# Loading and folding the first weights by quarters, with the first transposes in the softmax gap

## The chip, the cores and the metric

The kernel runs on one core of a Trainium2 chip. The time is the device time of one execution, in microseconds (us), from repeated executions; all of them here are marked "fast" (none is more than 1.5% above the fastest of its kernel). The traces give a span that is some 2 us shorter than the time (573.6 us for the kernel before), and all times of day below are counted from the start of that span. PE is the matrix engine (TensorE) and PEld its weight load, ACT is ScalarE, DVE is VectorE, POOL is GpSimd, which issues the loads. A "line" such as L345 is a line of that kernel's own source, so the same code has slightly different lines before and after.

## The reference, cut to what matters

```python
qn = q / (norm(q, axis=1) + 1e-6);  kn = k / (norm(k, axis=1) + 1e-6)   # q, k, v: 4 x 5824 x 256
A = softmax(kn.transpose(0, 2, 1) @ qn / tau)                          # 256 x 256, one per batch
x = (v @ A).reshape(23296, 256)
out = ((x @ w1) * (x @ w2) @ w3) @ w_out                               # w1, w2: 256 x 1024
```

The kernel uses that (v @ A) @ w1 equals v @ (A @ w1). It computes A for a batch, **folds** it into w1 and w2 (tiles `Wf`), and then multiplies rows of v by the folded weights. Before the first folds there is nothing for PE to do with v.

## The kernel before

A fold is two matmuls of 512 columns (over the two halves of the 256 contracted rows) and an eviction (a copy by ScalarE or VectorE out of PSUM, where the matmuls put their results) that scales by the reciprocal row sums. PSUM buffers carry tags: "ab" has four, "out" three, and each tag hands its buffers out in turn.

```python
def fold_mm(i, c2, tag="ab", on_act=None):
    ...                                              # w, c1, h from i; 512 columns
    nc.tensor.matmul(st["fold", i], lhsT=st["e"][:, c2, ...], rhs=w12[:, c2, w, h*512:(h+1)*512], ...)
    if c2 == CT - 1:                                 # evict, scaled: ScalarE or VectorE
        ...
def first_folds():
    sum_mm(0); fold_mm(0, 0); fold_mm(1, 0)          # need the first half of e
    sum_mm(1); fold_mm(0, 1); fold_mm(1, 1)          # need the second
    fold(2)
    transpose_half_on_pe(0, 0, 0, False)             # 8 transposes of v, tag "out"
    fold(3, on_act=True)
    fold(4, "out", on_act=False); fold(5, "out")
```

The loads behind q and k, all issued by GpSimd, and the end of the softmax:

```python
for h in range(2):                                   # w1, w2 by halves of 512 columns
    nc.gpsimd.dma_start(out=w12[:, :, 0, hs], in_=w1r[:, :, hs])
    nc.gpsimd.dma_start(out=w12[:, :, 1, hs], in_=w2r[:, :, hs])
    if h == 0: new_piece("v", 0, 0)
    load_part("v", 0, 0, h * half, (h + 1) * half)
load_piece("v", 0, 1); load_piece("v", 0, 2)
nc.gpsimd.dma_start(out=wout_sb, ...); nc.gpsimd.dma_start(out=w3_bf, in_=w3r)
...
soft0[3]()        # scaled scores and exp: gives e
busy(4)           # four filler matmuls
soft0[4]()        # first_folds
```

Everything later is placed by a planned clock: each piece of work has a planned time and cost, and is emitted between the products a = v Wf1 and b = v Wf2. Later loads also wait for earlier work: a one-element GpSimd copy ("gate", "hold") reads a tile, so that the loads after it are not issued before that tile is there.

```python
for i in range(2):
    at(1.5 + 0.6 * i, 0.43, soft0[5 + i])            # the last two folds, among the first products
```

Of the kernel before, what the change touches and what calls it, by code (L numbers as in the profile page):

```python
# [10 lines left out]
AF = mybir.ActivationFunctionType  # L11
ALU = mybir.AluOpType
F32 = DT.float32
BF16 = DT.bfloat16

P = 128
PIECE = 8
# [7 lines left out]
def kernel(  # L25
# [12 lines left out]
    nc = tc.nc  # L38
# [3 lines left out]
    F = moe_w1.shape[1]  # L42
# [6 lines left out]
    CT = C // P  # L49
# [18 lines left out]
    psum = ctx.enter_context(tc.tile_pool(name="psum", bufs=1, space=bass.MemoryType.PSUM))  # L68
# [15 lines left out]
    w12 = consts.tile([P, CT, 2, F], BF16)  # L84
# [15 lines left out]
    def new_piece(nm, n, pi):  # L100
        t = in_pool.tile([P, PIECE, C], BF16, tag=nm, name=f"{nm}_{n}_{pi}", bufs=IN_BUFS[nm])
        pieces[nm, n, pi] = t
        if pi == NP_ - 1:
            if nm != "v":
                nc.vector.memset(t[LEFT:, LAST, :], 0.0)
            nc.gpsimd.dma_start(out=t[:LEFT, LAST, :], in_=qk_main[nm, n][1])

    def load_part(nm, n, pi, lo, hi):
        nc.gpsimd.dma_start(  # L109
            out=pieces[nm, n, pi][:, lo:hi, :], in_=qk_main[nm, n][0][:, pi * PIECE + lo : pi * PIECE + hi, :]  # L110
        )

    def load_piece(nm, n, pi, cuts=()):

        new_piece(nm, n, pi)
        ends = [0, *cuts, LAST if pi == NP_ - 1 else PIECE]
        for lo, hi in zip(ends, ends[1:]):
            load_part(nm, n, pi, lo, hi)
# [3 lines left out]
    def new_vT(n):  # L122
        vTs[n] = (
            vT_pool.tile([P, NT - 1, CT, P], BF16, tag="vT", name=f"vT_{n}"),
            vT_pool.tile([P, CT, P + LEFT], BF16, tag="vTt", name=f"vTt_{n}"),
        )

    def pe_transpose(dst, src, tag, on_act):

        m = psum.tile([P, 8, P], BF16, tag=tag, name=f"tr_{nc.get_next_instruction_name()}", bufs={"ab": 4, "out": 3}[tag])  # L130
        for i, blk in enumerate(src):
            nc.tensor.transpose(m[:, i, :], blk, ident_b)
        if on_act:
            nc.scalar.copy(dst, m)
        else:
            nc.vector.tensor_copy(dst, m)

    def transpose_half_on_pe(n, pi, h, on_act):
        if pi == 0 and h == 0:
            new_vT(n)  # L140
        t = pieces["v", n, pi]
        i0 = 4 * h
        pe_transpose(
            vTs[n][0][:, pi * PIECE + i0 : pi * PIECE + i0 + 4, :, :].rearrange("p i c t -> p (i c) t"),
            [t[:, i0 + i, ct * P : (ct + 1) * P] for i in range(4) for ct in range(CT)],
            "out", on_act,
        )
# [17 lines left out]
    Wf = {}  # L165
# [39 lines left out]
    def busy(k):  # L205

        m = psum.tile([P, 512], F32, tag="ab", name=f"warm_{nc.get_next_instruction_name()}", bufs=4)
        for _ in range(k):
            nc.tensor.matmul(m, lhsT=warm[:, :P], rhs=warm, start=True, stop=True, skip_group_check=True)
# [29 lines left out]
    def soft_units(n):  # L239
        st = {}  # L240
# [93 lines left out]
            sum_mm(0)  # L334
            sum_mm(1)

        def fold_mm(i, c2, tag="ab", on_act=None):
            h, rest = divmod(i, 4)
            w, c1 = divmod(rest, 2)
            if c2 == 0:  # L340
                st["fold", i] = psum.tile(
                    [P, 512], F32, tag=tag, name=f"fold_{n}_{i}", bufs={"ab": 4, "out": 3}[tag]
                )
            nc.tensor.matmul(  # L344
                st["fold", i], lhsT=st["e"][:, c2, c1 * P : (c1 + 1) * P], rhs=w12[:, c2, w, h * 512 : (h + 1) * 512],  # L345
                start=(c2 == 0), stop=(c2 == CT - 1),
            )
            if c2 == CT - 1:
                dst = Wf[n][:, c1, w, h * 512 : (h + 1) * 512]
                if on_act if on_act is not None else i % 2 == 0:  # L350
                    nc.scalar.activation(out=dst, in_=st["fold", i], func=AF.Copy, scale=st["rs"][:, c1 : c1 + 1])  # L351
                else:
                    nc.vector.tensor_scalar_mul(dst, st["fold", i], st["rs"][:, c1 : c1 + 1])

        def fold(i, tag="ab", on_act=None):
            fold_mm(i, 0, tag)
            fold_mm(i, 1, tag, i % 2 == 0 if on_act is None else on_act)

        def first_folds():
            sum_mm(0)  # L360
            fold_mm(0, 0)
            fold_mm(1, 0)
            sum_mm(1)
            fold_mm(0, 1)
            fold_mm(1, 1)
            fold(2)
            transpose_half_on_pe(0, 0, 0, False)
            fold(3, on_act=True)
            fold(4, "out", on_act=False)
            fold(5, "out")  # L370

        if n == 0:
            return [k_first, k_row, q_first, scaled_first, first_folds] + [lambda i=i: fold(i) for i in range(6, 8)]
        head = [(0.0, norms), (0.5, k_row), (0.4, q_sums)]
        return head + [(0.0, scaled), (0.2, sums)] + [(0.43, lambda i=i: fold(i)) for i in range(8)]

# [13 lines left out]
    def at(t, cost, fn):  # L390
        seq[0] += 1
        agenda.append((t, seq[0], cost, fn))
# [105 lines left out]
    half = PIECE // 2  # L498
# [18 lines left out]
    w1r = moe_w1.rearrange("(ch cl) f -> cl ch f", cl=P)  # L517
    w2r = moe_w2.rearrange("(ch cl) f -> cl ch f", cl=P)
# [6 lines left out]
    soft0 = soft_units(0)  # L525
    whole = range(PIECE)
    lo, hi = range(half), range(half, PIECE)
# [10 lines left out]
        squares("q", pi, whole)  # L538
        products(pi, whole)
    load_piece("q", 0, 5, (1, 3, 4))  # L540
    for h in range(2):
        hs = slice(h * F // 2, (h + 1) * F // 2)
        nc.gpsimd.dma_start(out=w12[:, :, 0, hs], in_=w1r[:, :, hs])
        nc.gpsimd.dma_start(out=w12[:, :, 1, hs], in_=w2r[:, :, hs])
        if h == 0:
            new_piece("v", 0, 0)
        load_part("v", 0, 0, h * half, (h + 1) * half)
    load_piece("v", 0, 1)
    load_piece("v", 0, 2)
    nc.gpsimd.dma_start(out=wout_sb, in_=moe_w_out.rearrange("(lh ll) c -> ll lh c", ll=P))  # L550
# [14 lines left out]
        if i == 0:  # L565
            soft0[1]()
    soft0[3]()
    busy(4)
    soft0[4]()
    w_ready = [False]  # L570

# [15 lines left out]
    def make_agenda(b):  # L587
        agenda.clear()
        clock[0] = 0.0
        n = b + 1  # L590
        if b == 0:
            for i in range(2):
                at(1.5 + 0.6 * i, 0.43, soft0[5 + i])
            at(4.0, 0.5, lambda: transpose_half_on_pe(0, 0, 1, False))
            at(7.0, 0.5, lambda: transpose_half_on_pe(0, 1, 0, True))
            at(8.0, 0.5, lambda: transpose_half_on_pe(0, 1, 1, False))
            at(15.0, 0.0, transpose_w3)
            at(15.0, 0.0, lambda: transpose_piece(0, 2))
            for jt in range(FT):
                at(26.0 + 1.2 * jt, 0.87, lambda jt=jt: w_unit(jt))  # L600
            moves = [("v", 0, 3, 29.0), ("qk", 1, 0, 38.0), ("qk", 1, 1, 43.0), ("v", 0, 4, 50.0), ("qk", 1, 2, 58.0)]
            moves += [("qk", 1, 3, 63.0), ("v", 0, 5, 70.0), ("qk", 1, 4, 81.0), ("qk", 1, 5, 87.0)]
            moves += [("v", 1, 0, 96.0), ("v", 1, 1, 106.0), ("v", 1, 2, 116.0), ("qk", 2, 0, 126.0)]
            t0, t1 = 58.0, 120.0
        else:
            moves = [("v", b, 3, 1.0), ("qk", n, 1, 10.0), ("qk", n, 2, 17.0), ("v", b, 4, 26.0), ("qk", n, 3, 38.0)]
            moves += [("v", b, 5, 46.0), ("qk", n, 4, 58.0), ("qk", n, 5, 66.0)]
            moves += [("v", n, 0, 76.0), ("v", n, 1, 86.0), ("v", n, 2, 96.0), ("qk", n + 1, 0, 108.0)]
            moves = [m for m in moves if m[1] < B]
            t0, t1 = 16.0, 104.0  # L610

        before = (0, 2) if b == 0 else None
        for nm, m, pi, t in moves:
            if before is not None:
                at(t, 0.0, lambda w=before: hold(vTs[w[0]][1][:1, 0, :1] if w[1] == NP_ - 1 else vTs[w[0]][0][:1, w[1] * PIECE, 0, :1]))
            at(t, 0.0, gate)
            if nm == "qk":
                at(t, 0.0, lambda m=m, pi=pi: load_qk(m, pi))
                before = None
            else:  # L620
                at(t, 0.0, lambda m=m, pi=pi: load_piece("v", m, pi))
                at(t + 4.0, 0.0, lambda m=m, pi=pi: transpose_piece(m, pi))
                before = (m, pi)
        if n == B:
            agenda.sort()
            return
        units = score_units(n)
        for i, (cst, fn) in enumerate(units):
            at(t0 + (t1 - t0) * i / len(units), cst, fn)
        soft = soft_units(n)  # L630
        ts = [t1 + 1.0, t1 + 3.5, t1 + 4.0, t1 + 8.0, t1 + 12.0] + [t1 + 13.0 + 0.9 * i for i in range(8)]
        for t, (cst, fn) in zip(ts, soft):
            at(t, cst, fn)
        agenda.sort()
# [50 lines left out]
```

## Time and profile before

| | kernel before |
|---|---|
| time, median of the first three runs | 575.47 us (575.47 to 576.11) |
| span | 573.64 us |
| first softmax sum on PE | 37.00 us |
| first product a | 40.15 us |
| last wait of PE for a load | 32.66 us |

PE is busy for 98% of the span, and from 37.00 us on nearly without a hole. So the place to look is the order of its instructions near 37 us, which the prediction shows. These lines are from the timeline of GpSimd in the kernel before: start, duration, engine, line, operation, tiles, count.

```profile
29.73 0.70 POOL L543 DMA_DIRECT2D w<-in_moe_w_dram  x1 [0.73 <-DMA q<-in_q_dram]
30.42 0.72 POOL L544 DMA_DIRECT2D w<-in_moe_w_dram  x1
31.49 0.54 POOL L109 DMA_DIRECT2D v<-in_v_dram  x1 [0.35 <-DMA k<-in_k_dram]
...
35.19 0.93 POOL L550 DMA_DIRECT2D w_wout<-in_moe_w_out_dram  x1
```

The first halves of w1 and w2 are issued ahead of v, and w_out's issue, the first of the long ones, falls at 35.2 us, in the middle of the softmax.

### The profile page before, as it was taken

Reading aid. Unit: us, or ns where it says so; the run is one execution under the profiler, and the core shown is the slowest. Engines: PE = TensorE matmul, PEld = TensorE weight load, DVE = VectorE, ACT = ScalarE, POOL = GpSimd, SP = SyncE. Lnnn points to the kernel's source line nnn. Section 1 sums busy time; section 2 is a strip of 40 time slices with the busy share of each in tenths; the row PEclk is TensorE's granted clock in tenths of the full one; section 3 lists DMA queues with packets and bytes.
Section 4 is the critical chain, followed back from the end, with each engine's and each line's share of the span. In section 5 each row is a group of like instructions: output and inputs, shape, how many; then the busy total and the mean of one; then the engine's idle time right before and its main releaser. Section 6 shows DMA issues by size and latency. Waiting matters only on the chain.

```text
span 573.6 us, 10125 instructions
## 1 busy us (share of the span) xinstructions
PE 561.9 (98%) x3760; PEld 357.0 (62%) x3766; DVE 374.1 (65%) x597; ACT 337.9 (59%) x624; POOL 71.0 (12%) x162
## 2 busy tenths in 40 slices
PE   8789999999999999999999999999999999999997
PEld 4755576776666666666666666666665666666665
DVE  0047744787967567887776567778876656565564
ACT  0046534777766567776765567767765555454453
POOL 5240020202010111221000012021100000000000
PEclk9999999999999999999999999999999999999999
DMA  8999959779574696495661596675740325221011
GB/s 163 211 194 208 188 99 235 175 171 213 134 185 108 123 207 151 95 190 120 147 147 49 117 192 143 132 142 119 184 110 38 85 74 146 63 63 74 38 71 59
DMA packets 74561, 76.93 MB, mean 134 GB/s; under 512 B 54161, under 2 KB 58257, under 8 KB 74513
## 3 DMA queue, kind: packets, MB, share of 16 engines
q0 software_dynamic: 15504, 39.46, 39.2%
q1 hardware_dynamic: 58784, 36.64, 21.1%
q8 instruction: 29, 0.48, 0.3%
q10 hardware_dynamic: 224, 0.20, 0.1%
q14 instruction: 20, 0.16, 0.1%
HBM read 78.91 MB, written 23.86 MB: 179 GB/s over the span
## 4 chain that ended last, share of the span: by engine, by line
PE 91%; DMA 5%; ACT 1%; issue 1%; DVE 1%; POOL 1%; ACTq 0%; POOLq 0%
PE o L466 27%; PE a L425 27%; PE b L425 27%; PE G L188 5%; DMA k<-in_k_dram 3%; PE fold L344 2%; DMA q<-in_q_dram 2%; PE w L575 1%; ACT as L431 1%; POOL k L109 0%; PE row L272 0%; POOL q L109 0%; DVE abs L440 0%; DVE osb L487 0%; ACT kr L276 0%
## 5 line engine op out<-in xcount | busy, mean ns | idle before, releaser
L440 DVE TENSOR_TENSOR abs<-as,b 128x512 bf16<-128x512 bf16 x336 | 229.7, 685 | 140.5 <-ACT as L431 128.7
L431 ACT CAST as<-a 128x512 bf16<-128x512 f32 (+1 forms) x384 | 215.4, 562 | 177.7 <-PE a L425 86.7
L425 PEld LDWEIGHTS <-Wf 128*128 128x128 bf16 x1536 | 149.1, 98 | 102.5 <-issue 2.6
L466 PE MATMUL o<-W_sb,abs 128*128 128x256 bf16 x1376 | 209.7, 273 | 0.5 <-ACT osb L486 0.4
L425 PE MATMUL a<-vT,Wf 128*128 128x512 bf16 x704 | 209.4, 379 | 0.4
L425 PE MATMUL b<-vT,Wf 128*128 128x512 bf16 x704 | 209.4, 379 | 0.0
L466 PEld LDWEIGHTS <-abs 128*128 128x128 bf16 x1376 | 134.5, 98 | 82.0 <-issue 0.6
L197 DVE TENSOR_TENSOR acc<-acc,sq 128x1024 f32<-128x1024 f32 x66 | 80.4, 1219 | 0.8 <-ACT sq L185 0.8
L188 PE MATMUL G<-k,q 128*128 128x256 bf16 x276 | 49.6, 273 | 0.0
L185 ACT ACTIVATE sq<-q 128x512 f32<-128x512 bf16 x66 | 41.8, 633 | 0.0
L185 ACT ACTIVATE sq<-k 128x512 f32<-128x512 bf16 x66 | 41.6, 630 | 0.0
L413 POOL COPY gate_t<-abs 1x1 bf16<-1x1 bf16 x39 | 12.1, 310 | 183.7 <-DVE abs L440 183.1
L487 DVE COPY osb<-o 128x512 f32<-128x512 f32 x44 | 30.1, 684 | 0.0
L188 PEld LDWEIGHTS <-q 128*128 128x128 bf16 x276 | 27.0, 98 | 3.1
L486 ACT COPY osb<-o 128x512 f32<-128x512 f32 x44 | 25.7, 585 | 4.6 <-PE o L466 2.6
L417 POOL COPY gate_t<-vT 1x1 bf16<-1x1 bf16 x17 | 4.0, 234 | 180.5 <-DMA vT<-v 145.1
L274 ACT ACTIVATE kr<-row 128x256 f32<-128x256 f32 x4 | 1.5, 384 | 34.0 <-PE row L272 34.0
L109 POOL DMA_DIRECT2D q<-in_q_dram x29 | 15.6, 538 | 12.5 <-DMA k<-in_k_dram 5.2
L344 PE MATMUL fold<-w,e 128*128 128x512 bf16 x61 | 16.5, 378 | 0.1
L351 ACT ACTIVATE Wf<-fold,rs 128x512 bf16<-128x512 f32 x16 | 10.9, 687 | 7.2 <-PE fold L344 4.3
L109 POOL DMA_DIRECT2D k<-in_k_dram x25 | 13.7, 550 | 3.9 <-DMA k<-in_k_dram 1.9
L109 POOL DMA_DIRECT2D v<-in_v_dram x25 | 13.4, 539 | 4.0 <-issue 2.6
(87 smaller groups left out, 219.1 us busy)
## 6 DMA issues: line engine op xcount, KB each, us to landing
out_dram<-osb SPq DMA_DIRECT2D x44, 512.0 KB, 3.1
k<-in_k_dram POOLq DMA_DIRECT2D x19, 512.0 KB, 8.8
v<-in_v_dram POOLq DMA_DIRECT2D x19, 512.0 KB, 5.1
q<-in_q_dram POOLq DMA_DIRECT2D x18, 512.0 KB, 6.5
w_wout<-in_moe_w_dram POOLq DMA_DIRECT2D x1, 2048.0 KB, 22.9
k<-in_k_dram POOLq DMA_DIRECT2D x4, 320.0 KB, 9.4
v<-in_v_dram POOLq DMA_DIRECT2D x4, 320.0 KB, 5.2
q<-in_q_dram POOLq DMA_DIRECT2D x4, 256.0 KB, 11.9
```

The source lines that it names most:

```text
L109: nc.gpsimd.dma_start(out=pieces[nm, n, pi][:, lo:hi, :], in_=qk_main[nm, n][0][:, pi * PIECE + lo : pi * PIECE + hi, :])
L185: nc.scalar.activation(out=dst[:, :, part, :], in_=src[:, o : o + 2, :], func=AF.Square)
L188: nc.tensor.matmul(G[:, ct, :], lhsT=qt[:, i, ct * P : (ct + 1) * P], rhs=kt[:, i, :], start=(pr == 0 and part == 0 and ct == 0), stop=(pr ...
L197: nc.vector.tensor_add(accs[n], accs[n], sqs[0])
L344: nc.tensor.matmul(st["fold", i], lhsT=st["e"][:, c2, c1 * P : (c1 + 1) * P], rhs=w12[:, c2, w, h * 512 : (h + 1) * 512], start=(c2 == 0), ...
L413: nc.gpsimd.tensor_copy(gate_t, last_ab[0][:1, :1])
L425: nc.tensor.matmul(t[:, :n], lhsT=Wf[b][:, ct, w, j * P : (j + 1) * P], rhs=rhs_of(b, c, ct), start=(ct == 0), stop=(ct == CT - 1),)
L431: nc.scalar.copy(a_sb[:, :n], tiles[0][:, :n])
L440: nc.vector.tensor_mul(ab, a_sb, tiles[1])
L466: nc.tensor.matmul(tl[h][:, o, :], lhsT=lhsT, rhs=W_sb[:, j, :], start=(j == 0 and o == 0), stop=(j == FT - 1 and (small or o == 1)), skip ...
L486: nc.scalar.copy(o[:, 0:2, :], tl[0])
L487: nc.vector.tensor_copy(o[:, 2:4, :], tl[1])
```

## The change

Its intent: have v there earlier and transpose it while PE waits for the softmax; make the first folds, their evictions and their loads smaller, so that the first products can start sooner.

```diff
-        def fold_mm(i, c2, tag="ab", on_act=None):            # 512 columns
+        def fold_mm(key, c2, tag="ab", on_act=True):          # key = (w, c1, lo, hi)
...
         def first_folds():
             sum_mm(0)
-            fold_mm(0, 0); fold_mm(1, 0)
+            for c1 in range(CT): fold_mm((0, c1, 0, 256), 0)
             sum_mm(1)
-            fold_mm(0, 1); fold_mm(1, 1); fold(2)
-            transpose_half_on_pe(0, 0, 0, False)
-            fold(3, on_act=True)
-            fold(4, "out", on_act=False); fold(5, "out")
+            for c1 in range(CT): fold_mm((0, c1, 0, 256), 1, on_act=c1 == 0)
+            for w, lo in ((1, 0), (0, 256), (1, 256)):
+                for c1 in range(CT):
+                    for c2 in range(CT):
+                        fold_mm((w, c1, lo, lo + 256), c2, "ab" if lo == 0 else "out", c1 == 0)
...
-    for h in range(2): ...                                    # w halves, v between
+    new_piece("v", 0, 0)
+    load_part("v", 0, 0, 0, half)
+    for f0, f1 in ((0, 256), (256, 512), (512, F)):
+        nc.gpsimd.dma_start(out=w12[:, :, 0, f0:f1], in_=w1r[:, :, f0:f1])
+        nc.gpsimd.dma_start(out=w12[:, :, 1, f0:f1], in_=w2r[:, :, f0:f1])
+    load_part("v", 0, 0, half, PIECE)
...
-    busy(4)
+    busy(3)
+    transpose_half_on_pe(0, 0, 0, False)
     soft0[4]()
...
-            for i in range(2):
-                at(1.5 + 0.6 * i, 0.43, soft0[5 + i])
+            for i in range(4):
+                at(0.8 + 0.6 * i, 0.43, soft0[5 + i])
```

More of the change, by code (lines that the diff above doesn't have):

```diff
@@ L335, in sums @@
             sum_mm(1)
-        def fold_mm(i, c2, tag="ab", on_act=None):
-            h, rest = divmod(i, 4)
-            w, c1 = divmod(rest, 2)
+        def fold_mm(key, c2, tag="ab", on_act=True):
+            w, c1, lo, hi = key
             if c2 == 0:
-                st["fold", i] = psum.tile(
-                    [P, 512], F32, tag=tag, name=f"fold_{n}_{i}", bufs={"ab": 4, "out": 3}[tag]
+                st[key] = psum.tile(
+                    [P, 512], F32, tag=tag, name=f"fold_{n}_{w}_{c1}_{lo}", bufs={"ab": 4, "out": 3}[tag]
                 )
+            m = st[key][:, : hi - lo]
             nc.tensor.matmul(
-                st["fold", i], lhsT=st["e"][:, c2, c1 * P : (c1 + 1) * P], rhs=w12[:, c2, w, h * 512 : (h + 1) * 512],
+                m, lhsT=st["e"][:, c2, c1 * P : (c1 + 1) * P], rhs=w12[:, c2, w, lo:hi],
                 start=(c2 == 0), stop=(c2 == CT - 1),
@@ L348, in fold_mm, with fold @@
             if c2 == CT - 1:
-                dst = Wf[n][:, c1, w, h * 512 : (h + 1) * 512]
-                if on_act if on_act is not None else i % 2 == 0:
-                    nc.scalar.activation(out=dst, in_=st["fold", i], func=AF.Copy, scale=st["rs"][:, c1 : c1 + 1])
-                else:
-                    nc.vector.tensor_scalar_mul(dst, st["fold", i], st["rs"][:, c1 : c1 + 1])
-        def fold(i, tag="ab", on_act=None):
-            fold_mm(i, 0, tag)
-            fold_mm(i, 1, tag, i % 2 == 0 if on_act is None else on_act)
+                dst = Wf[n][:, c1, w, lo:hi]
+                if on_act:
+                    nc.scalar.activation(out=dst, in_=m, func=AF.Copy, scale=st["rs"][:, c1 : c1 + 1])
+                else:
+                    nc.vector.tensor_scalar_mul(dst, m, st["rs"][:, c1 : c1 + 1])
+        def fold(i, tag="ab"):
+            h, rest = divmod(i, 4)
+            w, c1 = divmod(rest, 2)
+            for c2 in range(CT):
+                fold_mm((w, c1, h * 512, (h + 1) * 512), c2, tag, i % 2 == 0)
         def first_folds():
             sum_mm(0)
-            fold_mm(0, 0)
-            fold_mm(1, 0)
+            for c1 in range(CT):
+                fold_mm((0, c1, 0, 256), 0)
             sum_mm(1)
-            fold_mm(0, 1)
-            fold_mm(1, 1)
-            fold(2)
-            transpose_half_on_pe(0, 0, 0, False)
-            fold(3, on_act=True)
-            fold(4, "out", on_act=False)
-            fold(5, "out")
+            for c1 in range(CT):
+                fold_mm((0, c1, 0, 256), 1, on_act=c1 == 0)
+            for w, lo in ((1, 0), (0, 256), (1, 256)):
+                for c1 in range(CT):
+                    for c2 in range(CT):
+                        fold_mm((w, c1, lo, lo + 256), c2, "ab" if lo == 0 else "out", c1 == 0)
         if n == 0:
-            return [k_first, k_row, q_first, scaled_first, first_folds] + [lambda i=i: fold(i) for i in range(6, 8)]
+            return [k_first, k_row, q_first, scaled_first, first_folds] + [lambda i=i: fold(i) for i in range(4, 8)]
         head = [(0.0, norms), (0.5, k_row), (0.4, q_sums)]
@@ L540 @@
     load_piece("q", 0, 5, (1, 3, 4))
-    for h in range(2):
-        hs = slice(h * F // 2, (h + 1) * F // 2)
-        nc.gpsimd.dma_start(out=w12[:, :, 0, hs], in_=w1r[:, :, hs])
-        nc.gpsimd.dma_start(out=w12[:, :, 1, hs], in_=w2r[:, :, hs])
-        if h == 0:
-            new_piece("v", 0, 0)
-        load_part("v", 0, 0, h * half, (h + 1) * half)
+    new_piece("v", 0, 0)
[4 more added lines that the diff above has]
+    load_part("v", 0, 0, half, PIECE)
     load_piece("v", 0, 1)
```

## The prediction

> **What bounds the kernel now.** I read the page's engine shares first, then who TensorE (PE) waited for, then the order of its work around the place that the change touches.
>
> ```profile
> PE 561.9 (98%) x3760; PEld 357.0 (62%) x3766; DVE 374.1 (65%) x597; ACT 337.9 (59%) x624; POOL 71.0 (12%) x162
> ...
> PE sqq L221 <- DMA q<-in_q_dram: 4.2, 4, 2.0
> PE warm_I-91_92 L209 <- DVE warm L78: 1.3, 1, 1.3
> PE sum L323 <- ACT e L307: 1.0, 1, 1.0
> PE o L466 <- ACT osb L486: 0.4, 1, 0.4
> ...
> 37.00:40.15 3.15, 3.15 (x24) 1.70 (x25) 2.00 (x5) 2.27 (x4) 0.18 (x1) 1.00 1.15 191
> 40.15:80.00 39.85, 39.85 (x240) 22.34 (x239) 26.98 (x42) 22.84 (x41) 0.90 (x3) 1.00 0.95 176
> ```
>
> The reader sees a PE that is busy for 98% of 573.6 us, and whose waits (us in total, times, longest) come almost all before 37 us: loads of q, the warm-up, and 1.0 us for the first softmax result e. From 37.00 us on (a row of stretches gives bounds, length, PE busy) it has no hole. So for the first 37 us loads and then a softmax chain set the pace; after that **the sum of PE's own instructions does**, and a microsecond more or less of PE work or PE waiting just after 37 us should move the end by as much. The change works exactly there:
>
> ```profile
> 34.98 1.03 PE L209 MATMUL warm_I-479_480<-warm 128*128 128x512 bf16 x3
> 37.00 0.20 PE L323 MATMUL sum<-ones_b,e 128*128 128x1 bf16 x2 [1.00 <-ACT e L307]
> 37.07 0.59 PE L344 MATMUL fold<-w,e 128*128 128x512 bf16 x2
> 37.50 0.19 PE L323 MATMUL sum<-ones_b,e 128*128 128x1 bf16 x2
> 37.55 1.02 PE L344 MATMUL fold<-w,e 128*128 128x512 bf16 x4
> 38.41 0.61 PE L132 MATMUL tr_I-508_509<-ident_b,v 128*128 128x128 bf16 x8
> 38.86 1.46 PE L344 MATMUL fold<-w,e 128*128 128x512 bf16 x6
> 40.15 0.59 PE L425 MATMUL a<-vT,Wf 128*128 128x512 bf16 x2
> ```
>
> Starts, not durations, are to be differenced, because matmuls overlap: 12 folds and 8 transposes stand between the softmax (37.00) and the first a (40.15). The transposes take 38.86 - 38.41 = 0.45 us of that, and one 512-column fold matmul 0.216 us (6 in 40.15 - 38.86).
>
> **What the Trainium skill says.** (1) "TensorE: Matmul & The Clock Gate", section "Wait — 56ns, not 53.3ns?": a warm matmul's start-to-start time is its columns at 2.4 GHz plus about 2.5 ns. Two of 256 columns then cost one of 512, less 2.5 ns the other way. The trace agrees: eight 256-column w matmuls advance the chain by 0.87 us, 0.109 each, against 0.216. (2) "DMA: Bandwidth & Descriptors", section "Why small descriptors are slow (HBM only)": a fixed cost per packet, which hurts most at the smallest sizes. In this trace a packet of 512 B takes 60 ns, of 1024 B 98 ns, of 2048 B 173 ns, so the fixed part shows; but see below, delivery hardly suffers. (3) "ScalarE: Activation LUTs", section "What ACT_TABLE_LOAD costs": an ACTIVATE takes 186 ns + 0.833 ns per column, about 93 ns more with a scale read from memory, and consecutive ones overlap by about 93 ns. For 512 columns that is 706 ns; the trace has 686. For 256 I subtract 256 x 0.833 = 213 from 686: **0.47 us**, one each 0.38 us. The trace's softmax exponentials of 256 columns, two in 0.91 us at 0.50 each, go at 0.41. (4) "Perfetto Trace Analysis", section "Optimization Strategy", says that consistent bubbles can mean too few buffers for the next tile; the kernel before shows none behind 37 us, the new one may.
>
> **Part by part.**
>
> *Transpose moved into the softmax gap.* One filler matmul of 0.216 us goes (four become three), and 8 transposes of 0.44 us enter. Fillers start at 34.98, so they end at about 35.63 and the transposes at 36.07, well ahead of e at 37.00, if v is there. The gap shrinks to some 0.9 us and the dense part loses **0.44 us**. VectorE's copy of the result (0.69 us) stands behind its second scaling (36.32 to 36.72), so from 36.7 to 37.4; it next works for the row sums at 37.7. Nothing is delayed.
>
> *Loads.* The issues of the kernel before keep eight transfers in flight: each waits for the landing of the eighth before it. Issue to landing, from the trace: first w1 half 29.73 to 34.7, first w2 half to 36.0, v half to 37.3, then 39.2, 40.5, 41.7. The last q piece lands at 33.5, and v half takes 1.3 us, so as the first it lands near 34.8, before 35.6. Is a quarter in 512-byte packets as cheap as half a half? The w_out load is 1024 such packets and landed in 49.3 - 46.6 = 2.65 us, 0.66 us per 256; halves of w need about 1.28. So quarters land at about 35.5, 36.1, 36.8 and 37.4, each ahead of its folds (37.07, 37.73, 38.2, 38.6). The second halves land at 38.7 to 40.5 and are wanted after 40. **Loads cost nothing**, and gain nothing: PE did not wait for w before either.
>
> *Folds.* The same columns are folded, so PE work is equal: 16 matmuls of 256 (1.73 us) in front, instead of 12 of 512 (2.6 us); 8 of 512 instead of 4 move behind the first a, 4 x 0.216 = 0.86 us. The first a comes earlier, but only by what is done later; with no wait it would start at 39.0, and the balance would be -0.44 us, plus 0.12 us for the second e, which is ready at 37.4 while the two first folds now end at 37.28: **-0.3 us**.
>
> *A new wait.* The last four small folds use the PSUM tag "out", which has three buffers. In order of allocation: k's squares 0, q's squares 1, transposes 2, row sums 0, then folds 1, 2, 0, **1**. The last fold must wait until ScalarE has emptied the first of them. Row sums end at 37.5, their reciprocal at 38.05, so ScalarE starts at 38.14, and that eviction is its third: 38.14 + 2 x 0.38 + 0.47 = 39.37, PE about 0.1 later (as e to sum). PE arrives at 37.51 + 12 x 0.108 = 38.81. So **+0.65 us** of waiting; before, only two folds used this tag, and none waited. First a at 39.7.
>
> *Four folds among the first products.* They come at planned clocks 0.8, 1.4, 2.0 and 2.6: one after the first pair a, b, two after the second, one after the third. Each takes one of four "ab" buffers and an eviction of 0.69 (ScalarE) or 0.75 us (VectorE), in a time when ScalarE already spends 0.585 and VectorE 0.685 us of each 0.866 us pair. Following the buffers by hand from a at 39.7: third b waits 0.1 us for the product of the second pair (about 43.1), and the last fold 0.3 us for the eviction of the second (about 43.85). Together **+0.4 us**. The fifth a starts at some 45.7, against 44.92 before.
>
> Sum: -0.44 + 0.12 + 0.65 + 0.4 = **+0.7 us**, and 575.47 + 0.7 = 576.2. I take 576.1, since hand-followed waits tend to come out a little long.
>
> **Rivals.** *A: the waits do not happen*, because evictions are faster than I think or buffers are given differently. Then -0.3 us, 575.2. For it: PE never waited in this stretch before. Against it: the buffer count is plain in the code. *B: small packets make loads the bound.* If a quarter took as long as a half (1.3 us), the fourth would land near 40.0 instead of 37.4, the first a would start at about 40.5, and later folds would wait for the halves at 41.8 and 43.1: +1.5 to +2.5 us, about 577.5. For it: 60 ns is more than half of 98. Against: the w_out load ran at nearly full rate. *C: v comes late* and PE, which works in order, holds the softmax sums behind the transposes. It would need v after 36.5, 1.7 us later than estimated; each us beyond costs one. *D: the delay is swallowed later.* PE's waits behind 40 us sum to under 1 us, so hardly.
>
> **Range and chances.** Every path lies between -0.4 and +2.5 us, and the three times of the kernel before spread by 0.64 us. I put 8 in 10 on 574.7 to 577.6. Two per cent is 11.5 us, twelve times any term here and three times the whole stretch from 37.00 to 40.15, so "within 2%" gets 0.985, slower 0.01 (B and C together and worse), faster 0.005.
>
> **What would show it.** In the changed trace: transposes before 37 us with VectorE's copy near 36.7; no PE wait for w or v; fold groups of 256 columns at 0.108 us; a wait of PE "fold" for ScalarE's eviction near 38.8, of about 0.65 us; first a near 39.7; further short waits until 45. If the first a starts near 39.0 with no such wait, rival A holds; if PE or its weight loads wait for a DMA between 35 and 44, B or C. Wrong altogether would be a change of over 3 us: that needs a disturbance outside this stretch, such as another order of loads delaying the later pieces of v or w3.

## The result, and the profile after

The changed kernel took 575.90 us (median of four, 575.72 to 576.03) against 575.55 us for the kernel before. The ratio is 1.0004 (95% interval 0.9986 to 1.0021): no difference that the times can tell from none. (A ratio is the mean time of one kernel's fast runs over that of the other's of the same rounds, so it is not quite the ratio of the medians.) The two traces tell more. Their spans are 574.26 and 573.64 us.

From the timeline of the changed kernel, around the same place as in the prediction's second extract:

```profile
34.60 0.81 PE L209 MATMUL warm_I-481_482<-warm 128*128 128x512 bf16 x2
...
35.25 0.61 PE L132 MATMUL tr_I-488_489<-ident_b,v 128*128 128x128 bf16 x8
...
36.63 0.20 PE L323 MATMUL sum<-ones_b,e 128*128 128x1 bf16 x2 [0.77 <-ACT e L307]
...
36.69 0.38 PE L345 MATMUL fold<-w,e 128*128 128x256 bf16 x2
...
37.03 0.20 PE L323 MATMUL sum<-ones_b,e 128*128 128x1 bf16 x2
...
37.09 1.67 PE L345 MATMUL fold<-w,e 128*128 128x256 bf16 x12
...
37.72 1.57 ACT L352 ACTIVATE Wf<-fold,rs 128x256 bf16<-128x256 f32 x4 [0.75 <-PE fold L345]
...
38.36 0.22 PEld L345 LDWEIGHTS <-e 128*128 128x128 bf16 x3 [0.30 <-DMA w<-in_moe_w_dram]
38.98 0.38 PE L345 MATMUL fold<-w,e 128*128 128x256 bf16 x2 [0.22 <-ACT Wf L352]
...
39.19 0.59 PE L427 MATMUL a<-vT,Wf 128*128 128x512 bf16 x2
```

The transposes do stand in the gap now. The first sum comes at 36.63 us, and the first a 2.57 us after it (from unrounded starts) instead of 3.15. But 14 small folds from 37.09 at 0.108 us each would end at 38.60, and a starts at 39.19: **0.59 us are lost**. The last two matmuls wait for an eviction by ScalarE, and just before them the weight load waited for the fourth quarter of w. The wait that the profile records, 0.22 us, is smaller, because it counts from the modelled end of the matmul before, and the next one could have started well ahead of that end. Differences of starts tell what is lost.

The first a being earlier is not yet a gain: two folds more come after it (0.86 us). A fairer mark is the start of ScalarE's copy of the ninth a, by which all folds and the same transposes are done in every version. From the first sum to there it takes 12.89 us in the kernel before and 13.33 in the changed one, **0.44 us more**. From the first sum to the end of the span it is 536.64 and 537.63, 0.99 us more; the sum itself came 0.37 us earlier, which gives the 0.62 us between the spans. PE's waits in the changed kernel show part of what was lost later; columns are the total, how often, the longest; G is the score product of the next batch, `as` ScalarE's copy of a.

```profile
PE sum L323 <- ACT e L307: 0.8, 1, 0.8
...
PE G L188 <- DMA k<-in_k_dram: 0.3, 1, 0.3
PE a L427 <- ACT as L433: 0.3, 1, 0.3
PE fold L345 <- ACT Wf L352: 0.2, 1, 0.2
```

The wait for k, 0.33 us at 142 us, is new: 100 us behind the change. The wait of 0.25 us for a copy by ScalarE, at 171.5 us, stands in place of one of 0.18 us at 182 us in the kernel before.

### The profile page after: what moved, and what is told of

Same layout as the page of the kernel before. It is cut to its first block, busy times and chain, and to the rows that moved or that the text cites. A ratio compares the mean times of both kernels' runs of the same rounds, so it can differ in the third digit from the quotient of the medians.

```text
span 574.3 us, 10145 instructions
## 1 busy us (share of the span) xinstructions
PE 562.3 (98%) x3767; PEld 357.5 (62%) x3773; DVE 374.8 (65%) x599; ACT 338.6 (59%) x626; POOL 73.7 (13%) x164
## 4 chain that ended last, share of the span: by engine, by line
PE 68%; ACT 1%; DVE 1%; issue 1%; ACTq 0%
PE o L468 21%; PE a L427 21%; PE b L427 21%; PE G L188 3%; PE fold L345 1%; ACT as L433 1%; DVE abs L442 0%; DVE osb L489 0%; ACT e L307 0%; PE row L272 0%; PE ss L283 0%; DVE oleft L483 0%; DVE rs L330 0%; DVE abs L444 0%; DVE rs L329 0%
## 5 line engine op out<-in xcount | busy, mean ns | idle before, releaser
L415 POOL COPY gate_t<-abs 1x1 bf16<-1x1 bf16 x39 | 13.6, 349 | 176.4 <-DVE abs L442 175.8
L345 PE MATMUL fold<-w,e 128*128 128x512 bf16 (+1 forms) x69 | 16.8, 354 | 0.3 <-ACT Wf L352 0.2
L352 ACT ACTIVATE Wf<-fold,rs 128x512 bf16<-128x512 f32 (+1 forms) x18 | 11.2, 640 | 8.0 <-PE fold L345 5.1
```

The costliest lines, as they stand in the source:

```text
L345: nc.tensor.matmul(m, lhsT=st["e"][:, c2, c1 * P : (c1 + 1) * P], rhs=w12[:, c2, w, lo:hi], start=(c2 == 0), stop=(c2 == CT - 1),)
L415: nc.gpsimd.tensor_copy(gate_t, last_ab[0][:1, :1])
```

## The experiments

Twelve runs were made, each beside runs of the kernel before on the same chip, in five rounds. No interval of any ratio excluded 1, and every median lies between 575.10 and 575.94 us, with 575.38 to 575.78 for the kernel before. Each trace is of one round alone, while the five rounds of one run differ by 0.31 us (x7_halves_tag) to 1.62 us (x3_tag): a wait that one trace shows need not be in the other rounds. The verdicts below therefore rest on the traces alone, read at these marks (all us; "from the sum" means from the first softmax sum on PE). "Ninth a copied" is the start of that copy. "Last early w" is the landing of the last piece of w that is needed before the first a.

| run | first sum | first a, from the sum | ninth a copied, from the sum | end, from the sum | last early w | w3 landed | wait for k at 142 | 128x2 addition |
|---|---|---|---|---|---|---|---|---|
| before | 37.00 | 3.15 | 12.89 | 536.64 | 39.18 | 59.16 | none | 0.16 |
| before_again | 36.72 | 3.15 | 12.89 | 536.61 | 38.83 | 59.14 | none | 0.41 |
| after | 36.63 | 2.57 | 13.33 | 537.63 | 38.32 | 60.71 | 0.33 | 0.16 |
| after_again | 36.44 | 2.57 | 13.25 | 537.05 | 38.02 | 59.44 | none | 0.16 |
| x1_halves | 37.20 | 2.56 | 13.24 | 537.01 | 37.19 | 59.65 | none | 0.58 |
| x2_clock | 36.69 | 2.71 | 13.31 | 537.89 | 38.90 | 61.14 | 0.72 | 0.16 |
| x3_tag | 36.76 | 2.41 | 13.09 | 536.84 | 38.67 | 60.42 | none | 0.16 |
| x4_moveonly | 36.71 | 3.62 | 13.36 | 537.08 | 39.40 | 59.39 | none | 0.58 |
| x5_tag_held | 36.65 | 2.68 | 13.39 | 537.62 | 38.83 | 61.32 | 0.29 | 0.16 |
| x6_move_held | 36.74 | 3.17 | 12.91 | 536.63 | 38.98 | 59.70 | none | 0.16 |
| x7_halves_tag | 37.07 | 2.06 | 12.74 | 536.57 | 37.79 | 59.47 | none | 0.58 |
| x7_again | 37.27 | 1.99 | 12.67 | 536.46 | 37.26 | 59.46 | none | 0.58 |
| x8_held | 36.97 | 1.99 | 12.66 | 536.48 | 37.09 | 59.20 | none | 0.16 |
| x8_again | 36.75 | 1.99 | 12.66 | 536.74 | 37.27 | 60.11 | 0.08 | 0.16 |

The last column is a tiny instruction on the softmax chain, explained with x6.

### Both kernels once more

> The kernel before once more, unchanged: first sum between 36.6 and 37.2 us by chance of the first loads, first a 3.15 us after it, no wait for k behind 37 us, w3 landing near 59.2 us; its time shows what two sets of runs of one kernel differ by (up to 0.1%).

> The changed kernel once more, unchanged, to see which waits recur. Theory L (late loads): the w3 load lands 1 us or more later than in the kernel before, and the wait for k near 142 us is there again or nearly (0 to 0.7 us); first a 2.5 to 2.7 us after the first sum. Theory of chance: the wait is gone with w3 as late.

The kernel before repeats to 0.03 us from its first sum to its end, but the sum itself came 0.28 us earlier: the loads of the first 33 us differ from run to run. In the changed kernel the first a repeats exactly and the ninth to 0.09 us, but the wait for k was gone this time, with w3 landed at 59.44 instead of 60.71 us. Its end lay 0.44 us further from the sum than in before_again. So the loss near the change is steady, and the one at 142 us comes and goes with the loads. Times: 575.69 us for after_again, 575.49 for before_again.

### Undoing the quarter loads, and the planned clock (x1, x2)

```diff
-    for f0, f1 in ((0, 256), (256, 512), (512, F)):
+    for f0, f1 in ((0, 512), (512, F)):                       # x1_halves
```

> The changed kernel with one thing undone: w1 and w2 loaded again in halves of 512 columns (v half still ahead of them); the folds stay quartered. Theory L (the late losses come from the slower loads: in the changed kernel w3 landed at 60.7 us against 59.2, which pushed the next v, q and k loads back by 1.5 to 3 us and left matrix engine waits of 0.33 us for k at 142 and 0.25 us near 171): w3 lands at about 59.5, the v load behind it starts near 73.3 instead of 74.8, and the waits at 142 and 171 are gone; span 0.5 us shorter than that of the changed kernel. Rival P (the planned clock of the program, which runs 0.86 us ahead because four folds and not two are charged, shifts the loads): w3 may land earlier, but the waits at 142 and 171 stay. Both: the wait of the last small fold for its buffer stays, first a 2.55 us after the first sum.

```diff
-                at(0.8 + 0.6 * i, 0.43, soft0[5 + i])
+                at(0.8 + 0.6 * i, 0.215, soft0[5 + i])        # x2_clock
```

> The changed kernel with the planned cost of the four later folds at 0.215 instead of 0.43 each, so that the program's planned clock adds the same 0.86 us as before; the same instructions, in another order from the third product on. Theory P: the waits at 142 us for k (0.33) and near 171 (0.25) vanish, span 0.5 us shorter. Theory L: w3 still lands near 60.7 and the waits, or others of the same size, remain.

With halves, w3 landed at 59.65, the next load of v was issued at 73.39 instead of 74.80 us, and the wait for k was gone; from the sum to the end it took 0.62 us less than in after (the span was no shorter, since the sum came 0.58 us later; and after_again, with quarters, took 537.05 us to x1's 537.01). As expected the first a stayed where it was (2.56), though the weights were all there by 37.19 us: the fold's buffer alone is enough to hold it. PE's waits in x1_halves:

```profile
PE fold L345 <- ACT Wf L352: 0.4, 1, 0.4
```

The planned clock is not the cause of that wait. With the clock restored the wait for k was longest of all:

```profile
PE G L188 <- DMA k<-in_k_dram: 0.7, 1, 0.7
PE fold L345 <- DMA w<-in_moe_w_dram: 0.5, 1, 0.5
```

Over all fourteen traces the wait for k is 0.29 to 0.72 us in exactly the three where w3 landed after 60.5 us (60.71, 61.14, 61.32), 0.08 in one where it landed at 60.11, and absent in the ten others, one of them with 60.42. Each of those three traces is of the slowest round of its run (576.03, 576.36 and 576.04 us), so the other rounds, of which there are no traces, may have been without it. The way from a late w3 to this wait is read from the code and not tested alone, and the size of the wait does not follow w3's lateness: the transposes of w3 follow its landing, those of v's third piece follow them, and a hold on these keeps the next loads of v, q and k back; in after, v by 1.5 us. With quarters and no hold on w3 (four traces) w3 landed at 59.4 to 61.1 us, with halves (four of the changed orders) at 59.4 to 59.7. So quarters tend to make it later, though one of their four traces (59.44) does not show it. In after, 0.92 of the 1.55 us by which w3 is later than in the kernel before are already there when the first piece of v is complete (42.63 against 41.71 us), behind the quarters; the rest comes at the third piece of v (48.14 against 46.63), and why is open. The wait of 0.25 us at 171 us is another matter, and here theory L fails: it stayed in x1_halves, and is there in every trace whose planned clock runs ahead, whereas the kernel before, x2_clock, x4_moveonly and x6_move_held have 0.18 us at 182 us instead. It comes with the order of the program, which the planned clock sets (restored alone, in x2_clock, it takes this wait away), and costs only 0.07 us more than what it replaces (see below).

### The buffer of the last small fold (x3)

```diff
-                        fold_mm(..., c2, "ab" if lo == 0 else "out", c1 == 0)
+                        fold_mm(..., c2, "ab" if lo == 0 or (w, c1) == (1, 1) else "out", c1 == 0)
```

> The changed kernel with the last small fold in the buffers of a and b instead of the three of out, so that it need not wait for the eviction of the first fold there. Theory S (the buffer is what holds the first a back): the first a starts 0.3 to 0.6 us earlier, 1.97 to 2.25 us after the first sum instead of 2.56. Rival D (the late fourth quarter of w, which landed at 38.3 us, holds it anyway): not below 2.25 us, and a wait of the weight loads for the DMA is what shows. Time 0.2 to 0.6 us less than the changed kernel's if the gain is kept.

The first a came only 0.16 us earlier, 2.41 us after the sum, as this text's rival D said (not below 2.25). The wait for the eviction is gone and one for the load takes its place:

```profile
PE fold L345 <- DMA w<-in_moe_w_dram: 0.2, 1, 0.2
```

The fourth quarter landed at 38.67 us in this run. So two waits lay on top of each other, and taking the later one away uncovers the other. From the sum to the end it took 536.84 us, less than both traces of the changed kernel, but the median time, 575.94 us, does not show the expected gain.

### Both at once (x7)

```diff
     # x1_halves and x3_tag together
```

> The changed kernel with both suspected waits removed: w1 and w2 loaded in halves (second half-load of 37.2 us instead of a last quarter at 38 to 39 us) and the last small fold in the buffers of a and b. If the buffer and the late quarter together are the whole of what holds the first a back, it starts 1.97 us after the first sum (2.56 in the changed kernel, 2.41 with the buffer alone, 2.56 with the halves alone), and the time from the first sum to the end of the span is 536.3 to 536.5 us (536.6 in the kernel before, 537.1 and 537.6 in the changed one). A rival third wait, for evictions by ScalarE or VectorE, would keep the first a or the first b at least 0.3 us later.

> The same kernel a second time, to see whether it repeats: from the first sum to the first a within 0.1 us, from there to the end within 0.3 us, since late waits for k came and went by chance between two profiles of the changed kernel.

From PE's timeline in x7_halves_tag:

```profile
37.07 0.20 PE L323 MATMUL sum<-ones_b,e 128*128 128x1 bf16 x2 [1.19 <-ACT e L307]
...
37.53 1.76 PE L345 MATMUL fold<-w,e 128*128 128x256 bf16 x14
39.13 0.59 PE L427 MATMUL a<-vT,Wf 128*128 128x512 bf16 x2
```

All 14 folds run through (but for 0.08 us in this run, where the second half-load landed only at 37.79), and the first a starts 2.06 and 1.99 us after the sum; 1.97 was expected. To the end it took 536.57 and 536.46 us, where 536.3 to 536.5 was expected. There is no third wait of the size of 0.3 us. The ninth copy comes 0.15 and 0.22 us sooner than in the kernel before: that is what is left of the 0.44 us of transposes when both waits are gone. But the first sum came late, at 37.07 and 37.27 us, with a wait for e of 1.19 us instead of 0.77.

### The move alone (x4), and later issues of w_out and w3 (x5, x6)

```diff
     # x4_moveonly, on the kernel before
+    new_piece("v", 0, 0); load_part("v", 0, 0, 0, half)       # ahead of the w halves
...
-            transpose_half_on_pe(0, 0, 0, False)              # in first_folds
...
-    busy(4)
+    busy(3)
+    transpose_half_on_pe(0, 0, 0, False)
```

> The kernel before with only the move: v half loaded first, its transposes in the softmax gap, one filler less; w in halves and folds of 512 as before. If the move is worth what the 8 transposes take, the first a starts 2.70 us after the first sum instead of 3.15 and the time falls by 0.44 us. The rival: the second half of w1, which landed at 39.2 us just as its fold began in the kernel before, is now wanted 0.44 us earlier and becomes a wait of 0.2 to 0.4 us, so that the first a starts only 0.05 to 0.25 us earlier.

The rival won, and by more than it asked for: the second half of w1 landed at 39.40 us, PE waited, and the first a came 0.47 us later than in the kernel before. By starts, six folds from 37.25 us at 0.216 us end at 38.55, and the seventh started at 39.45: 0.90 us lost for 0.44 gained. By this trace the move needs the smaller front, or fewer folds in it, to be worth anything. The times do not say so: x4's median of 575.10 us is the lowest of all runs, against 575.78 for the kernel before in the same rounds (ratio 0.9990, 0.9976 to 1.0004), and the traced round, 575.57 us, was the slowest of its five. So how often this wait comes is not shown.

Why do the pieces of w land so late? In every trace something slows them between 35 and 39.5 us: in the changed kernel the first three quarters land 0.7 to 0.8 us apart, the fourth 1.67 us after the third. The last number of a row of stretches, GB/s, shows it; first the kernel before, then the changed one:

```profile
core 0: us, PE busy (x) PEld busy (x) DVE busy (x) ACT busy (x) POOL busy (x), PEclk, DMA share, GB/s
35.00:39.50 4.50, 3.45 (x26) 1.68 (x25) 2.97 (x12) 3.12 (x9) 2.00 (x3) 1.00 1.13 181
...
35.00:39.50 4.50, 3.46 (x31) 2.23 (x31) 3.37 (x13) 3.07 (x9) 3.55 (x6) 1.00 1.05 140
```

Over all fourteen traces, the rate in this stretch was 137 to 159 GB/s in the five traces with quarters and 171 to 185 in the nine with halves. So the slow spell is in all of them, and deeper with quarters. GpSimd issues the long loads of w_out and w3 at that time, so I held these back:

```diff
+            at(0.5, 0.0, gate)            # x5_tag_held: x3_tag with this; x6_move_held: x4_moveonly with this
+            at(0.5, 0.0, load_w3)         # the issues of w_out and w3, after the first product
```

> The changed kernel with the last small fold in the buffers of a and b, and with the issues of w_out and w3 held until the first product of a and b is there (about 41 us) instead of 36.7 to 38.5. In every run so far single packets took up to 1.7 us between 35 and 39.5 us, whatever their size, while GpSimd issued these two long loads, and the fourth quarter of w landed at 38.3 to 38.9 us, 0.7 to 0.9 us later than the packets' usual pace gives. Theory I (issuing those loads slows the transfers then under way): the fourth quarter lands by 37.6, the fold's wait for it is gone, and the first a starts 2.0 us after the first sum. Rival E (something else of that time, such as the evictions' own writes, slows them): the quarter lands at 38.3 or later and the first a stays at 2.4. If I holds, span from the first sum to the end about 536.4 us against 536.6 of the kernel before.

> The kernel before with v first, the transposes in the gap, and the same hold of w_out and w3. Theory I: the second half of w1 lands by 38.3 instead of 39.4, the fold's wait of 0.74 us is gone or under 0.1, and the first a starts 2.70 us after the first sum (3.62 without the hold, 3.15 in the kernel before); then the move is worth its 0.44 us to the end. Rival E: the half lands near 39.4 and the wait of 0.7 us stays.

**That theory falls.** The fourth quarter landed at 38.83 us in x5_tag_held, later than without the hold, and the second half of w1 at 38.98 in x6_move_held, where 38.3 was expected. (It was 39.40 in x4_moveonly, but 39.18 and 38.83 in two traces of the kernel before, so this shift is no more than repeats differ by; the rate in x5, 142 GB/s, was no better either.) The wait in x6 shrank to 0.45 us by starts, which eats up the 0.44: its ninth copy is at 12.91, the kernel before's at 12.89. In x5 w3, held back, landed last of all runs.

The hold had another effect. A VectorE instruction between the norms and e, the addition of 1e-6 to a tile of 128x2, is the last column of the table. In x4_moveonly, without the hold:

```profile
34.97 0.94 POOL L549 DMA_DIRECT2D w_wout<-in_moe_w_out_dram  x1
...
35.33 0.58 DVE L293 TENSOR_SCALAR r<-r 128x2 f32<-128x2 f32 x1
```

The addition ends at 35.91, exactly with the issue of w_out. In x6_move_held that issue comes at 42.14 us:

```profile
35.78 0.16 DVE L293 TENSOR_SCALAR r<-r 128x2 f32<-128x2 f32 x1
```

PE's wait for e fell from 1.19 to 0.78 us. The fourteen traces agree: from the end of PE's last score product to the first sum it takes 1.86 or 1.87 us in the nine where the addition took 0.16 us, 2.11 in the one where it took 0.41, and 2.29 in the four where it took 0.58. The page "SBUF — State Buffer" of the Trainium skill, section "Who interferes with whom", says that a VectorE tensor_scalar in a two-port mode and GpSimd share a pair of SBUF ports, and that whoever comes second is blocked for the whole of the other's instruction. The trace agrees in what can be seen: the addition was long in the five traces where w_out's issue began before it and outlasted its start by over 0.3 us, and 0.16 us in the others; in the kernel before it began 0.07 us ahead of the issue's end and was not held visibly. Whether this small addition runs in such a mode no trace shows. And in the changed kernel it ran in 0.16 us (at 35.67) under the issues of three v loads (35.13 to 36.78), so not every issue blocks; what sets w_out's apart stays open.

### A version without any of the three (x8)

```diff
     # x7_halves_tag, and:
     soft0[4]()
+    hold(Wf[0][:1, 0, 0, :1])            # w_out and w3 are issued after the first eviction
+    nc.gpsimd.dma_start(out=wout_sb, ...); nc.gpsimd.dma_start(out=w3_bf, in_=w3r)
```

> The version of the two last runs (v first, w in halves, quartered folds, last small fold in the buffers of a and b), with the loads of w_out and w3 issued only when the first folded weights are there (about 38 us). In ten of ten profiles the 128x2 addition in the softmax chain on VectorE took 0.16 us where GpSimd was not issuing w_out in its middle and 0.41 or 0.58 us in the five where it was, ending with that issue. Theory G (that issue holds VectorE's instruction up): the addition takes 0.16 us, PE waits 0.77 us for e instead of 1.19, and the first sum comes at 36.6 to 36.9 us instead of 37.1 to 37.3; first a 2.0 us after it; span 573.0 to 573.4 us. Rival: chance of the loads; the addition takes 0.58 us again or the first sum stays at 37.1 or later. Cost to watch: w3 lands later, 60 to 61 us, and may bring the wait for k near 142 us (0 to 0.4 us).

> The same once more: the addition at 0.16 us again, first sum within 0.3 us of the first time, first a 2.0 us after it; median time 0.2 to 0.7 us under that of the kernel before, which five rounds may not separate from none.

(The count in that text is wrong: there were twelve profiles then, seven with 0.16 us and five with 0.41 or 0.58.) The addition took 0.16 us both times, in x8_held at

```profile
36.02 0.16 DVE L293 TENSOR_SCALAR r<-r 128x2 f32<-128x2 f32 x1
```

and PE waited 0.77 us for e. The first sum came at 36.97 and 36.75 us, the first a 1.99 us after it, and w3 landed at 59.20 and 60.11 us, with no wait for k in x8_held. The spans were 573.45 and 573.50 us, not under 573.4 as I had expected. In x8_held the first sum missed its range (36.6 to 36.9) because PE's last score product ended late, at 35.10 us (34.42 to 35.14 over all traces, by chance of the loads); in x8_again the sum was in its range and the wait for k made the difference. x8_again lost 0.25 us more than x8_held by starts, all of it at the wait for k at 141 us, of which the profile records 0.08. Times: 575.26 and 575.29 us against 575.38 of the kernel before in the same rounds, ratios 0.9996 (0.9984 to 1.0009) and 0.9994 (0.9980 to 1.0008). The medians are the right way round, by 0.12 and 0.09 us where 0.2 to 0.7 was expected, but **this is not shown to beat the kernel before**; by its marks it gains some 0.2 us in the folds and 0.4 us where the issue of w_out would have hit the addition, as in x7.

## Why the prediction was right or wrong

The time was 575.9 us where 576.1 was predicted, within the range, and the class was right. That the number fits so well is partly luck: of the 0.62 us between the two spans, 0.44 are of the kind foreseen, a wait for k that was not foreseen added 0.49, and a first sum 0.37 us earlier, not foreseen either, took off nearly as much; in the second pair of traces the spans differ by 0.16 us. The steps fared differently.

- **Transposes into the gap, -0.44 us: right.** They ran at 35.25 us, VectorE's copy at 36.27, and the dense part lost them. With the waits gone (x7, x8) the ninth copy came 0.15 to 0.23 us sooner; the sum of the terms that stay there, -0.44 + 0.12 + 0.08, is -0.24.
- **The second half of e, +0.12: right.** Two small folds from 36.69 end at 36.91, and the second sum starts at 37.03.
- **The buffer of the last small fold, +0.65: right**, 0.59 by starts. Of these some 0.19 us were lost one fold earlier, to the fourth quarter; in x1_halves, without that, 0.58 us were lost at the buffer. The eviction took 0.475 us (0.47 expected). x1_halves shows that it is enough alone, x7 that it and the late quarter are all.
- **Four folds among the first products, +0.4: mis-sized.** By starts the first of them was late by 0.10 us, and that was a load (the second half of w1 landed at 40.10), and the last by 0.08. The wait of 0.1 us for a product did not come. With this term at 0.18 the sum is +0.45, and the ninth copy measured +0.44 and, in the second trace, +0.36.
- **"Loads cost nothing": wrong.** The step that failed is "quarters land at about 35.5, 36.1, 36.8 and 37.4". The first three came slightly sooner (35.11, 35.91 and 36.65 us in the changed kernel), but the fourth came at 38.0 to 38.9 us in five traces, the second half of w1 at 40.10 in the changed kernel. The cost was hidden behind the buffer in the changed kernel, and is bare in x3 and x5. Rival B is half right. Single packets were not slower as a rule: the median one of 512 B took 60 ns, as before, and the loads in halves had a slow spell too. But with quarters the whole rate was lower there, 137 to 159 against 171 to 185 GB/s. The packet size alone does not explain it, since w_out's load, of the same 512 B, took 2.71 us in the changed kernel (48.14 to 50.85) and 2.65 before; smaller transfers in flight and more issues by GpSimd at that time are rivals that no run separates. Single packets took up to 1.66 us there, that one of 1024 B and so not of a quarter; that such packets are the cause is not shown. Holding the issues of w_out and w3 back did not cure it, and the trace does not tell which of the 16 DMA engines a packet was on.
- **"Further short waits until 45": not far enough.** The prediction looked at later stages only for a way to swallow a delay (its rival D), and had none that adds to it, but for its last sentence, which names later pieces of v or w3 as a way to a loss of over 3 us. In one of two traces the later w3 made PE wait for k at 142 us, 0.33 us as recorded. The starts of ScalarE's copies of a in the two traces of the changed kernel differ by 0.49 us more behind that point than ahead of it. From 161 us to the last copy the changed kernel loses 0.07 us more against the kernel before, by the starts of the same copies: the wait at 171 us in place of the one at 182. So 0.44 + 0.49 + 0.07 = 1.00, for 0.99 us to the end, and in the second pair of traces 0.36 + 0.07 = 0.43 of 0.44.
- **The start of the dense part, taken as fixed at 37.00: wrong.** It lay, over all traces, between 36.44 and 37.27 us. Most of that is chance of the loads, since PE's last score product ended between 34.42 and 35.14, but the changed order also moved w_out's issue from about 35.1 to 36.6 us, out of the way of the addition. Compared with before_again that is 0.25 us, and it helped to keep the net small.

So most of the expected 0.44 us was given back at once by a PSUM buffer with a late load just under it. The net effect of a few tenths of a microsecond, on 575 with a spread of as much, can be read in traces and not in times.

## What to carry to other kernels

When work is cut finer, count the buffers of the tag that the pieces pass through: here one piece more than buffers put an eviction on the path, and removing that wait may only uncover a load below it, so test the two together. A load that is late without being waited for can still move later loads through gates and holds, and show up a hundred microseconds on. Compare traces from a mark that both kernels share, and by starts, before believing either a gain or a loss under one part in a thousand.

## What the Trainium skill lacked or had wrong

- "SBUF — State Buffer", "Who interferes with whom", has the rule of the shared ports. It lacks a measure for a VectorE instruction that a DMA issue holds up: here a 128x2 tensor_scalar of 0.16 us took 0.58 us under the issue of w_out (0.94 us) and ended with it, in four traces (0.41 us in a fifth), and 0.16 us under the issues of v loads of about 0.58 us.
- "DMA: Bandwidth & Descriptors", "Why small descriptors are slow (HBM only)", gives the cost per packet. It does not say what a mix of loads then delivers. Here the median packet of 512 B stayed at 60 ns, but between 35 and 39.5 us 137 to 159 GB/s were moved in the five traces with such loads of w, and 171 to 185 in the nine without. What is behind that stays open.
- "ScalarE: Activation LUTs", "What ACT_TABLE_LOAD costs": its numbers give an estimate of 186 + 93 + 213 = 492 ns for an eviction of 256 columns with a scale from memory; the trace has 475, from PSUM.
